# Attention and two expert layers on one core: q turned in pairs of 64-row transposes, half of k's exps taken from PSUM, first loads reordered

## The chip, the core and the metric

The kernel runs on one core of a Trainium2 chip. The core has a matrix engine (TensorE, here PE; PEld is its loading of stationary operands), VectorE (DVE), ScalarE (ACT), GpSimd (POOL) and SyncE (SP), each with an instruction stream of its own that is worked off strictly in order; they meet only at semaphores. Sixteen DMA engines move data between HBM and the on-chip memory SBUF. PE writes its results to PSUM, eight banks of 128 x 512 fp32, from where DVE and ACT read them. The metric is the device time of one execution in microseconds (us); lower is better.

## The reference

Three stages in a row, all in fp32, with 8 batches, 8 heads, 576 positions, 64 values per head. The change touches the first alone:

```python
def phi(x):
    proj = np.einsum('bhsd,df->bhsf', x, w_phi)                   # 128 features
    proj = proj - np.max(np.abs(proj), axis=-1, keepdims=True)
    return np.concatenate([np.exp(proj), np.exp(-proj)], axis=-1)
q_p, k_p = (phi(q), phi(k))
kv = np.einsum('bhsf,bhsd->bhfd', k_p, v)
z = np.sum(k_p, axis=2)
num = np.einsum('bhsf,bhfd->bhsd', q_p, kv)
den = np.einsum('bhsf,bhf->bhs', q_p, z)[..., None] + 1e-06
return (num / den).astype(np.float32)
```

Its result passes through two expert layers (a mixing of each position with the one before it, four matrix products with w_k, w_v, w_r and w_val, a convolution of width 5, a product with w_out).

## The kernel before

The attention runs in 32 steps, `j = 2n + p`. A group `n` holds four heads: a step works on two of them, `ab` = 0 and 1, which lie on partitions 0 to 63 and 64 to 127 of the loaded q and k, and on their first 512 positions in 4 chunks of 128. The last 64 positions of all four heads are done once per group (`tails`, `turn_tails`). For each step:

- `proj` (L630, called by `q_proj` and `k_proj`): PE multiplies 4 chunks of each head with w_phi, the two heads on the two 64-row halves of the array at once, each into a PSUM bank of its own (`project`, L618). `centre` (L621) then has DVE take the largest absolute value of each row (L624) and subtract it (L626) into SBUF.
- for k, ACT takes exp of the centred values and of their negatives, 512 columns at a time (L670), into `ek`.
- for q, `turn` (L677) transposes each head's 4 chunks on the whole 128x128 array (L683), one bank per head, and ACT takes the two exps on the way from PSUM to SBUF (L687), into `qe`.
- `kv` (L704): PE sums exp(k) times v (with a column of ones for z) on the two 64-column halves of the array (L724); ACT copies the result (L369).
- `num` (L734), once per head: PE multiplies q's exps with that state (L758), again on column halves; ACT copies; `scale` divides on POOL and DVE; `back` (L788) transposes the result on the whole array (L798).

Meanwhile the weights of the expert layers are fetched, rearranged by ACT, DVE and POOL and written back to HBM (`convert`). After the last step come the expert layers, with products on the whole array (L900).

In the trace every fp32 product of the attention shows as two weight loads and two matmuls, a transpose as one of each; so the 4 chunks of two heads are 16 pieces of L618, and a turn of one head 4 of L683.

The order on each engine is not written out. `Order.run` (L166) gives every task a duration and a due time: it is `j` plus a number from the table `T` (L33). For each engine it takes the task that can start first, by the durations written in the code (0.84 for a projection, `t_act(n)` for ACT and so on; `ENTER` is what it books for a change of the array's shape, `SOON` and `EARLY` how far it goes to avoid one). It also chooses the PSUM banks. The instructions are then issued in that order; on the chip each engine goes through its list and waits where a semaphore is not yet there. PE's order, for example, can't change at run time.

The first loads: SP issues q's three pieces for group 0 (512, 128 and 512 columns), then v; ACT issues w_phi in two halves and then k's three pieces (`load_t`, L584, with `by="ACT"`). PE runs 8 products on the identity as a warm-up until they land.

Of the kernel before, what the change touches and what calls it, by code (L numbers as in the profile page):

```python
# [22 lines left out]
QW = 1152  # L23
# [9 lines left out]
T = dict(load_q=-1.89, load_k=-2.75, load_v=-2.03, tails=-1.0, q_proj=-1.5, k_proj=-1.505, turn=-0.592, sums=-0.5, num=0.4, back=1.049, finish=1.9, convert=1.09, ones=-1.23)  # L33
FROM, TO = 0, 27.43
# [9 lines left out]
DMA_END = 2.5  # L44
# [3 lines left out]
KV = 0.117  # L48
ENTER = {"rows": 0.2, "columns": 0.14, "all": 0.15}
SOON, EARLY = 0.6, 0.405  # L50
# [241 lines left out]
def build(ctx, tc, qt, kt, vv, wphi, mu, wk, wr, wv, wval, cw, wout, out):  # L292
# [49 lines left out]
    def ps(tag):  # L342
        return Buf(tag, None)
# [240 lines left out]
    def load_t(n, dst, src, nm):  # L584

        f = sb(nm + "h", [128, QW])
        cuts = [(0, 512), (1024, QW), (512, 1024)] if n == 0 else [(0, QW)]
        for i, cut in enumerate(cuts):
# [41 lines left out]
    def proj(x, j, tag):  # L630
# [8 lines left out]
        add("PE", 0.84, lambda: project(bs, x[n], [p * 512 + 128 * i for i in range(4)], 0),  # L639
# [3 lines left out]
        return [d[:2] for d in ds]  # L643

    def tails(j):
# [8 lines left out]
        add("PE", 0.42, go, r=cols_of(qs[n], n, 2) + cols_of(ks[n], n, 2) + [("wph", 0), ("wph", 1)], w=bs, new=bs, split="rows")  # L654
# [9 lines left out]
    def k_proj(j):  # L664
        ds = proj(ks, j, "d")
        for ab in range(2):
            d, tok = ds[ab]
            e = st[j]["ek", ab] = sb("ek", [128, 4, 2, 128])
            for half in range(2):
                add("ACT", t_act(512, False), lambda d=d, e=e, half=half: act(  # L670
                    out=e[:, :, half], in_=d(), func=AF.Exp, scale=-1.0 if half else 1.0),
                    r=[tok], w=[(e, half)] if j or ab + half < 2 else [(e, half), "first"], new=[] if half else [e])

# [3 lines left out]
    def turn(j, ab):  # L677

        s = st[j]
        if ab == 0:  # L680
            s["qe"] = sb("qe", [128, 2, 2, 512])
# [4 lines left out]
        for half in range(2):  # L686
            add("ACT", t_act(512), lambda half=half: act(  # L687
                out=e[:, ab, half, :], in_=b[:], func=AF.Exp, scale=-1.0 if half else 1.0),
                r=[b], w=[(e, ab, half)], new=[] if ab or half else [e])
# [44 lines left out]
    def num(j, ab):  # L734
# [9 lines left out]
        reads = [(e, ab, 0), (e, ab, 1), s["kv"]]  # L744
# [551 lines left out]

    for j in range(NP):
        n, p = divmod(j, 2)
        st[j] = {}
        if p == 0:  # L1300
            due(j + T["load_q"] if n else -8.0, load_t, n, qs, qt, "q")
            due(j + T["load_k"] if n else -7.0, load_t, n, ks, kt, "k")
            due(j + T["load_v"] if n else -6.0, load_v, n)
            due(j + T["ones"] if n else -4.0, ones, n)
            due(j + T["tails"], tails, j)
        due(j + T["q_proj"], q_proj, j)
        due(j + T["k_proj"], k_proj, j)
        if p == 0:
            due(j + T["turn"] + 0.4, turn_tails, n)
# [64 lines left out]
```

## Time and profile before

| | |
|---|---|
| median of 3 runs | 957.3 us (952.86 to 958.5) |
| profiled execution | 957.62 us, of which the span of the core is 955.8 us |
| TensorE clock granted over the span | 1.000 of full speed |
| PE busy | 933.7 us (98%) |
| DVE, ACT, POOL busy | 831.3 (87%), 690.6 (72%), 204.3 us (21%) |

The attention fills the first third of the span: POOL, which works only there, is idle from the 14th of the page's 40 slices on, and PE issues its first product of the expert layers at 305.36 us. A busy PE means that a matmul is somewhere in its pipeline, so two pieces overlap in the busy sums, and their cost is better read from when the next piece begins (the chain in order of time). ACT's and DVE's neighbours overlap too: two in a row take less than twice the time of one.

### The profile page before, as it was taken

How to read it: one execution, taken by the hardware profiler on the slowest of the kernel's cores; microseconds unless marked ns; L12 is line 12 of the kernel's file. 1: busy time of each engine (PE TensorE's matmuls, PEld its weight loads, DVE VectorE, ACT ScalarE, POOL GpSimd, SP SyncE). 2: the span in 40 equal slices, each digit the busy share in tenths (PEclk: the TensorE clock that was granted, in tenths of full speed). 3: DMA queues.
4: the chain of work that ended last, by engine and by line, in shares of the span. 5: the costliest groups of instructions: out<-in, count | busy, mean ns of one | idle time of the engine just before them, and what ended most of it. 6: DMA issues, size and time to landing. Idle time of an engine off the chain costs nothing.

```text
span 955.8 us, 27000 instructions
## 1 busy us (share of the span) xinstructions
PE 933.7 (98%) x11264; PEld 906.8 (95%) x11264; DVE 831.3 (87%) x1276; ACT 690.6 (72%) x1253; POOL 204.3 (21%) x360
## 2 busy tenths in 40 slices
PE   6999999999999999999999999999999999999997
PEld 6899989988898999999999999999999999999997
DVE  5899989989887799879978978997997897899695
ACT  4768778777677987668857947876885794787453
POOL 0296978777683000000000000000000000000000
PEclk9999999999999999999999999999999999999999
DMA  7465589889857475588378577748837856754883
GB/s 242 155 203 184 175 272 306 258 283 305 286 170 263 155 275 204 182 274 295 118 284 287 189 259 260 246 181 288 293 128 275 285 200 252 267 193 165 285 306 138
DMA packets 79770, 224.27 MB, mean 235 GB/s; under 512 B 10144, under 2 KB 35104, under 8 KB 66592
## 3 DMA queue, kind: packets, MB, share of 16 engines
q1 hardware_dynamic: 70352, 212.45, 64.9%
q10 hardware_dynamic: 9296, 10.09, 3.0%
q8 instruction: 89, 1.46, 0.6%
q14 instruction: 33, 0.27, 0.1%
HBM read 186.87 MB, written 35.65 MB: 233 GB/s over the span
## 4 chain that ended last, share of the span: by engine, by line
PE 88%; DVE 5%; ACT 4%; DMA 2%; issue 1%; ACTq 0%; DVEq 0%
PE c L900 58%; PE b L724 8%; PE b L618 8%; PE b L758 8%; PE b L683 4%; PE b L798 2%; DVE ops L372 1%; ACT ops L878 1%; DMA out<-y 1%; DVE x L869 1%; DMA ops<-in_kt 1%; ACT y L878 0%; ACT x L878 0%; ACT g L878 0%; PE b L696 0%
## 5 line engine op out<-in xcount | busy, mean ns | idle before, releaser
L900 PE MATMUL c<-ops,u 128*128 128x288 f32 x1968 | 275.5, 295 | 4.1 <-DVE ops L372 2.5
L900 PEld LDWEIGHTS c<-ops,u 128*128 128x128 f32 x1968 | 266.2, 188 | 6.1 <-DVE ops L372 3.4
L900 PE MATMUL c<-ops,wkt 128*128 128x288 f32 x1344 | 180.0, 295 | 0.7 <-ACT c L1021 0.7
L900 PEld LDWEIGHTS c<-ops,wkt 128*128 128x128 f32 x1344 | 178.3, 188 | 1.1 <-ACT c L1021 0.9
L624 DVE TENSOR_REDUCE dd<-b 128x4 f32<-128x512 f32 (+1 forms) x160 | 95.0, 627 | 25.8 <-PE b L618 24.4
L872 DVE SCALAR_TENSOR_TENSOR g<-x,cwt,g 128x576 f32<-128x576 f32 x128 | 102.1, 815 | 0.0
L878 ACT ACTIVATE ops<-k 128x576 fp32r<-128x576 f32 x96 | 65.3, 680 | 46.2 <-PE c L900 43.2
L372 DVE TENSOR_TENSOR ops<-k,ops 128x576 fp32r<-128x576 f32 x96 | 71.7, 755 | 25.2 <-ACT ops L878 25.0
L618 PE MATMUL b<-wph,ops 64*128 64x128 f32 x1152 | 83.2, 287 | 6.3 <-DMA ops<-in_kt 4.7
L618 PEld LDWEIGHTS b<-wph,ops 64*128 64x128 f32 x1152 | 71.2, 191 | 14.6 <-issue 5.5
L687 ACT ACTIVATE y<-b 128x512 f32<-128x512 f32 x128 | 69.9, 599 | 13.4 <-PE b L683 12.3
L758 PE MATMUL b<-g,y 128*64 128x65 f32 x2176 | 74.9, 223 | 1.4 <-issue 1.4
L758 PEld LDWEIGHTS b<-g,y 128*64 128x64 f32 x2176 | 68.0, 137 | 7.3 <-issue 3.4
L369 ACT ACTIVATE x<-b 128x260 f32<-128x260 f32 (+3 forms) x96 | 40.3, 424 | 38.9 <-PE b L758 27.2
L878 ACT ACTIVATE k<-k 128x576 f32<-128x576 f32 x98 | 63.3, 679 | 0.9 <-DVE k L869 0.5
L878 ACT ACTIVATE sp<-c 128x576 f32<-128x576 f32 x50 | 32.4, 648 | 43.3 <-PE c L900 43.3
L626 DVE TENSOR_TENSOR k<-b,dd 128x512 f32<-128x512 f32 (+1 forms) x84 | 49.5, 616 | 0.0
L900 PE MATMUL c<-y,u 128*128 128x288 f32 x336 | 48.0, 294 | 0.0
L900 PE MATMUL c<-y,xf 128*128 128x288 f32 x336 | 46.8, 295 | 0.0
L900 PEld LDWEIGHTS c<-y,u 128*128 128x128 f32 x336 | 45.7, 188 | 0.0
L900 PEld LDWEIGHTS c<-y,xf 128*128 128x128 f32 x336 | 45.3, 188 | 0.0
L878 ACT ACTIVATE k<-c 128x576 f32<-128x576 f32 x64 | 41.3, 646 | 5.0 <-PE c L900 4.5
(148 smaller groups left out, 1795.2 us busy)
## 6 DMA issues: line engine op xcount, KB each, us to landing
u<-ws SPq DMA_DIRECT2D x86, 1024.0 KB, 5.4
xf<-ws SPq DMA_DIRECT2D x16, 1024.0 KB, 6.5
ws<-dd SPq DMA_DIRECT2D x28, 512.0 KB, 6.2
dd<-ws SPq DMA_DIRECT2D x24, 512.0 KB, 5.7
ot<-ws SPq DMA_DIRECT2D x20, 512.0 KB, 5.9
xs<-x SPq DMA_DIRECT2D x16, 576.0 KB, 4.3
xx<-xs SPq DMA_DIRECT2D x8, 1152.0 KB, 7.6
out<-y ACTq DMA_DIRECT2D x32, 288.0 KB, 5.4
```

The costliest lines, as they stand in the source:

```text
L369: act(out=out, in_=x, func=AF.Copy)
L372: eng.tensor_tensor(out=out, in0=x, in1=hi.bitcast(F32), op=ALU.subtract)
L618: mm(out=bs[ab][:, (at + i) * 128:(at + i + 1) * 128], lhsT=x[r, c:c + 128], rhs=wph[r], start=True, stop=True)
L624: add("DVE", t_dve(128 * n), lambda: nc.vector.tensor_reduce(out=m[:, 0:n, 0], in_=b3[:, 0:n], axis=AX.X, op=ALU.max, apply_absolute_value ...
L626: add("DVE", t_dve(128 * n), lambda: tt(out=d[0](), in0=b3[:, 0:n], in1=m[:, 0:n].to_broadcast([128, n, 128]), op=ALU.subtract), r=[b, m], ...
L683: add("PE", 0.109 * 4, lambda: [nc.tensor.transpose(out=b[:, c * 128:c * 128 + 128], in_=d()[:, c], identity=ident) for c in range(4)], r= ...
L687: add("ACT", t_act(512), lambda half=half: act(out=e[:, ab, half, :], in_=b[:], func=AF.Exp, scale=-1.0 if half else 1.0), r=[b], w=[(e, a ...
L724: mm(out=b[y, o:o + 65], lhsT=lhs[:, y], rhs=vt[:, a:a + 65], start=(k == 0), stop=(c == 3), skip_group_check=True)
L758: mm(out=b[rows, at:at + 65], lhsT=lhs, rhs=a[:, o:o + 65], start=(k == 0), stop=(half == 1), skip_group_check=True)
L872: add("DVE", d_time(n) + 0.06, lambda: stt(out=out(), in0=x(), scalar=scalar(), in1=y(), op0=ALU.mult, op1=ALU.add), r=r, w=w)
L878: act(out=out(), in_=x(), func=func, **more)
L900: mm(out=o[:, half, 0:TB], lhsT=a, rhs=mov[b][c], start=first and k == 0, stop=last and k == n - 1, skip_group_check=True)
```

## The change

Three edits of the code, and a new table of due times with them.

1. `turn` handles both heads at once. A head's chunk, 128 positions by 128 features, is transposed in two halves of 64 positions (`y`), the lower 64 partitions on the lower half of the array's rows, the upper on the upper half. The halves go to two banks: bank `y` gets that half of both heads. There are 16 transposes of 64 x 128 instead of 8 of 128 x 128; the exps are still four of 512 columns, now by half instead of by head, so `num` of one head needs all four. The turn waits for both heads of q.
2. `proj_k` replaces `k_proj`. For head `ab` = 0 nothing changes. For `ab` = 1 (`ASIDE`) DVE takes the maximum and its negative (4 columns), and does not subtract: ACT reads the projection from PSUM and adds the maximum as a per-partition bias, so the exps go chunk by chunk, 8 of 128 columns in place of 2 of 512.
3. The three pieces of k and q for group 0 are issued on SP, alternating, k first; v comes between the first two pieces and the third.

```diff
-T = dict(load_q=-1.89, load_k=-2.75, load_v=-2.03, tails=-1.0, q_proj=-1.5, k_proj=-1.505, turn=-0.592, ...
+T = dict(load_q=-1.801, load_k=-2.905, load_v=-2.62, tails=-0.979, q_proj=-1.5, k_proj=-1.505, turn=-0.592,
...
-DMA_END = 2.5
+DMA_END = 2.574
...
+TURN = 0.47
+ASIDE = ((0, 1), (1, 1))
 ENTER = {"rows": 0.2, "columns": 0.14, "all": 0.15}
-SOON, EARLY = 0.6, 0.405
+SOON, EARLY = 0.211, 0.35
...
         for i, cut in enumerate(cuts):
+            if n == 0 and i != part:
+                continue
             c, wide = slice(*cut), cut[1] - cut[0]
-            load(lambda c=c: f[:, c], lambda c=c: src[n, :, c], wide * 512, w=[(f, i)], new=[] if i else [f],
-                 by="ACT" if (n, nm) == (0, "k") else "SP")
+            load(lambda c=c: f[:, c], lambda c=c: src[n, :, c], wide * 512, w=[(f, i)], new=[] if i else [f])
...
-        add("PE", 0.84, lambda: project(bs, x[n], [p * 512 + 128 * i for i in range(4)], 0),
+        add("PE", 0.893, lambda: project(bs, x[n], [p * 512 + 128 * i for i in range(4)], 0),
...
+    def proj_k(j):
...
+        for ab in range(2):
+            e = st[j]["ek", ab] = sb("ek", [128, 4, 2, 128])
+            if (p, ab) in ASIDE:
+                apart(bs[ab], e, j, ab)
+            else:
...
+    def apart(b, e, j, ab):
+        m, b3 = sb("m", [128, 2, 4]), Part(lambda: b[:].rearrange("p (c f) -> p c f", f=128))
+        add("DVE", t_dve(512), lambda: nc.vector.tensor_reduce(
+            out=m[:, 0], in_=b3[:], axis=AX.X, op=ALU.max, apply_absolute_value=True), r=[b], w=[m], new=[m])
+        add("DVE", 0.15, lambda: nc.vector.tensor_scalar(
+            out=m[:, 1], in0=m[:, 0], scalar1=-1.0, scalar2=None, op0=ALU.mult), w=[m])
+        for half in range(2):
+            def go(half=half):
+                for c in range(4):
+                    act(out=e[:, c, half], in_=b3[:, c], func=AF.Exp, scale=-1.0 if half else 1.0,
+                        bias=m[:, 1 - half, c:c + 1])
+            add("ACT", 4 * t_act(128) - 0.3, go, r=[b, m], w=[(e, half)] if j or ab + half < 2 else [(e, half), "first"],
+                new=[] if half else [e])
...
-    def turn(j, ab):
+    def turn(j):
...
-        b, (d, tok), e = ps("qp"), s["dq"][ab], s["qe"]
-        add("PE", 0.109 * 4, lambda: [nc.tensor.transpose(
-            out=b[:, c * 128:c * 128 + 128], in_=d()[:, c], identity=ident) for c in range(4)],
-            r=[tok], w=[b], new=[b])
...
+        bs, ds = [ps("qp"), ps("qp")], s["dq"]
+        e = s["qe"] = sb("qe", [128, 2, 2, 512])
+
+        def go():
+            for ab in range(2):
+                for c in range(4):
+                    for y in range(2):
+                        r, k = slice(64 * y, 64 * y + 64), 256 * ab + 64 * c
+                        nc.tensor.transpose(out=bs[y][:, k:k + 64], in_=ds[ab][0]()[r, c], identity=ident[r, r])
+
+        add("PE", TURN, go, r=[tok for _, tok in ds], w=bs, new=bs, split="rows")
...
-        reads = [(e, ab, 0), (e, ab, 1), s["kv"]]
+        reads = [(e, y, half) for y in range(2) for half in range(2)] + [s["kv"]]
...
-                lhs = e[:, h, half, 128 * c + 64 * y:128 * c + 64 * y + 64] if c is not None else ex[:, half, h, rows]
+                lhs = e[:, y, half, 256 * h + 64 * c:256 * h + 64 * c + 64] if c is not None else ex[:, half, h, rows]
...
-            due(j + T["load_q"] if n else -8.0, load_t, n, qs, qt, "q")
-            due(j + T["load_k"] if n else -7.0, load_t, n, ks, kt, "k")
...
+                for i in range(3):
+                    due(-8.0 + 1.5 * i, load_t, n, qs, qt, "q", i)
+                    due(-8.5 + 1.5 * i, load_t, n, ks, kt, "k", i)
+                due(-5.7, load_v, n)
```

With the new durations and due times the planner sets another order. PE in the middle of the attention, before: `b_..` are PSUM banks, `wph,ops` is w_phi with the loaded q or k, `ident,sp` the turn of one head, `u,k` and the like the state product, `ident,ot` the transposes of `back`.

```order
L618 MATMUL b_82<-wph,ops 128x128
L618 MATMUL b_90<-wph,ops 128x128
L683 MATMUL b_83<-ident,sp 128x128 x4
L724 MATMUL b_89<-u_72,k_69 64x65 x8
L724 MATMUL b_89<-u_72,u_70 64x65 x16
L724 MATMUL b_89<-u_72,g 64x65 x16
L798 MATMUL b_91<-ident,ot 128x128 x4
L798 MATMUL b_81<-ident,ot 128x128
L683 MATMUL b_88<-ident,sp 128x128 x4
L618 MATMUL b_84<-wph,ops 128x128
```

The two heads' turns stand apart, each on the whole array, one of them alone between a projection and a state product. PE in the middle of the attention, after (`g,y` is `num`, `ident,k` the turn of the tails):

```order
L760 MATMUL b_89<-u_72,k_69 64x65 x24
L760 MATMUL b_89<-u_72,u_70 64x65 x16
L794 MATMUL b_90<-g,y 64x65 x24
L732 MATMUL b_84<-ident,k_69 128x128 x2
L794 MATMUL b_83<-g,y 64x65 x16
L627 MATMUL b_88<-wph,ops 128x128
L627 MATMUL b_89<-wph,ops 128x128
...
L718 MATMUL b_90<-ident,sp 128x64
L718 MATMUL b_82<-ident,sp 128x64
```

Both heads' turn (16 rows of L718, alternating between two banks) now stands in one place, here directly behind a projection that uses the same row halves. ACT in the first steps, before: `u<-k` and `k<-k` are exps of k, `g<-b` and `x<-b` copies of kv and num, `y<-b` exps of q.

```order
L670 ACTIVATE k_69<-k_69 128x4x128 x2
L670 ACTIVATE u_70<-k_69 128x4x128 x2
L369 ACTIVATE g<-b_84 128x260
L369 ACTIVATE x_74<-b_90 128x260
L687 ACTIVATE y<-b_88 128x512 x2
```

A step's four exps of k are four instructions. ACT in the first steps, after:

```order
L667 ACTIVATE k_69<-k_69 128x4x128 x2
L680 ACTIVATE u_70<-b_91,dd 128x128 x8
L375 ACTIVATE g<-b_90 128x260
L375 ACTIVATE x_74<-b_82 128x260
L416 ACTIVATE xf<-xx 128x512
L723 ACTIVATE y<-b_81 128x512 x2
```

The second pair has become eight that read a PSUM bank, ahead of the same copies. SP's first issues, after (`in_kt`, `in_qt`, `in_vv` are k, q and v in HBM; before, SP has q's three pieces first, then v, and k's stand behind w_phi on ACT):

```order
L396 DMA ops<-in_kt 128x512
L396 DMA ops<-in_qt 128x512
L396 DMA ops<-in_kt 128x128
L396 DMA ops<-in_qt 128x128
L396 DMA u_71<-in_vv 128x1040
L396 DMA u_71<-in_vv 64x2x64 x2
L396 DMA ops<-in_kt 128x512
L396 DMA ops<-in_qt 128x512
```

k's first piece has moved from the third place of ACT's queue to the first of SP's, and the third pieces of k and q stand behind v.

## Rows read from the trace of the kernel before

**Rows 1.** the page, parts 1 and 4: busy time and the chain by engine:
```profile
PE 933.7 (98%) x11264; PEld 906.8 (95%) x11264; DVE 831.3 (87%) x1276; ACT 690.6 (72%) x1253; POOL 204.3 (21%) x360
...
PE 88%; DVE 5%; ACT 4%; DMA 2%; issue 1%; ACTq 0%; DVEq 0%
```

**Rows 2.** windows: us, busy us (instructions) of PE, PEld, DVE, ACT, POOL; clock:
```profile
25.00:305.00 280.00, 275.06 (x6227) 252.12 (x6228) 251.70 (x467) 209.67 (x460) 199.49 (x337) 1.00 0.74 242
```

**Rows 3.** waits of PE, 25:305 us (total, times, longest), first and last of three:
```profile
PE b L758 <- issue: 2.9, 2, 1.5
...
PE b L724 <- issue: 1.4, 2, 0.8
```

**Rows 4.** chain in order of time: start us, us, line and pieces:
```profile
1.95 7.71 DMA ops<-in_kt
...
94.79 2.33 PE b L724 x80
...
98.06 1.02 PE b L683 x8
99.08 1.99 PE b L618 x32
...
143.96 2.48 PE b L724 x80
146.45 0.59 PE b L683 x4
...
148.77 1.09 PE b L618 x16
...
155.60 2.02 PE b L758 x64
```

**Rows 5.** timeline, start and first expert product: start us, us, engine:
```profile
0.72 1.19 ACTq L390 DMA_DIRECT2D wph<-in_wphi  x2
...
1.34 3.78 PE L566 MATMUL b<-ident 128*128 128x128 f32 x16 [1.34 <-POOL ident masks.py:199]
...
9.80 5.00 PE L618 MATMUL b<-wph,ops 64*128 64x128 f32 x56 [4.68 <-DMA ops<-in_kt]
...
305.36 1.86 PE L900 MATMUL c<-ops,wkt 128*128 128x288 f32 x12
```

**Rows 6.** groups by line and form, 25 to 305 us, weight loads:
```profile
L758 PEld LDWEIGHTS b<-g,y 128*64 128x64 f32 x2165 | 67.6, 137 | 7.2 <-issue 3.4 <-ACT x L369 0.2 <-ACT x L700 0.2
L618 PEld LDWEIGHTS b<-wph,ops 64*128 64x128 f32 x1048 | 63.6, 187 | 9.4 <-issue 5.3 <-ACT x L369 1.8 <-ACT k L670 0.2
...
L683 PEld LDWEIGHTS b<-ident,sp 128*128 128x128 f32 x248 | 27.1, 141 | 3.1
```

**Rows 7.** DMA issues, 0 to 25 us: KB each, median us to landing:
```profile
ops<-in_qt SPq DMA_DIRECT2D x2, 256.0 KB, 3.7
```

**Rows 8.** groups on DVE and ACT, last two from 305 us on:
```profile
L626 DVE TENSOR_TENSOR k<-b,dd 128x512 f32<-128x512 f32 x59 | 38.7, 679 | 0.0
...
L670 ACT ACTIVATE u<-k 128x512 f32<-128x512 f32 x60 | 34.6, 628 | 2.0 <-DVE k L626 2.0
...
L369 ACT ACTIVATE x<-b 128x128 f32<-128x128 f32 x15 | 4.1, 276 | 1.5 <-PE b L798 1.5
...
L878 ACT ACTIVATE k<-k 128x576 f32<-128x576 f32 x98 | 63.3, 679 | 0.9 <-DVE k L869 0.5
...
L878 ACT ACTIVATE dd<-xx,mut 128x576 f32<-128x576 f32 x32 | 23.6, 766 | 0.0
```

**Rows 9.** timelines of DVE and of ACT in one step:
```profile
111.10 0.27 DVE L777 RECIPROCAL g<-dd 128x8 f32<-128x8 f32 x2
...
126.16 1.14 ACT L670 ACTIVATE u<-k 128x512 f32<-128x512 f32 x2
```

**Rows 10.** waits of ACT, 25 to 305 us, the two largest:
```profile
ACT x L369 <- PE b L758: 24.6, 28, 1.9
ACT y L687 <- PE b L683: 11.3, 21, 2.5
```

More of the change, by code (lines that the diff above doesn't have):

```diff
@@ L30 @@
 LEAST, MOST = pattern((896 + 128) << 20), pattern(((1150 + 128) << 20) | 0xFFFFF)
[L33 to L34 removed]
+T = dict(load_q=-1.801, load_k=-2.905, load_v=-2.62, tails=-0.979, q_proj=-1.5, k_proj=-1.505, turn=-0.592,
+         sums=-0.5, num=0.4, back=1.078, finish=1.924, convert=1.09, ones=-2.309, turn_x=0.434, turn_step=0.308,
+         num_step=0.301, scale=0.526)
+ODD = dict(q_proj=0.038, k_proj=-0.02, turn=0.0, sums=0.0, num=-0.15, back=0.0)
+FIRST = dict(q_proj=0.649, k_proj=0.226, tails=0.378, turn=0.044, sums=0.765)
+FROM, TO = 0, 27.413
 LAST = ("pj", "qp", "kv")
@@ L643, in proj @@
         return [d[:2] for d in ds]
+    def proj_k(j):
+        n, p = divmod(j, 2)
+        bs = [ps("pj"), ps("pj")]
+        add("PE", 0.893, lambda: project(bs, ks[n], [p * 512 + 128 * i for i in range(4)], 0),
+            r=cols_of(ks[n], n, p) + [("wph", 0), ("wph", 1)], w=bs, new=bs, split="rows")
+        for ab in range(2):
[3 more added lines that the diff above has]
+            else:
+                d = sb("d", [128, 4, 128])
+                centre(bs[ab], (lambda d=d: d[:], d, [d]), 4)
+                for half in range(2):
+                    add("ACT", t_act(512, False), lambda d=d, e=e, half=half: act(
+                        out=e[:, :, half], in_=d[:], func=AF.Exp, scale=-1.0 if half else 1.0),
+                        r=[d], w=[(e, half)] if j or ab + half < 2 else [(e, half), "first"], new=[] if half else [e])
+    def apart(b, e, j, ab):
[4 more added lines that the diff above has]
+            out=m[:, 1], in0=m[:, 0], scalar1=-1.0, scalar2=None, op0=ALU.mult), w=[m])
+        for half in range(2):
+            def go(half=half):
[4 more added lines that the diff above has]
+                new=[] if half else [e])
     def tails(j):
@@ L652, in go @@
                 project(bs, x[n], [1024], i)
-        add("PE", 0.42, go, r=cols_of(qs[n], n, 2) + cols_of(ks[n], n, 2) + [("wph", 0), ("wph", 1)], w=bs, new=bs, split="rows")
+        add("PE", 0.446, go, r=cols_of(qs[n], n, 2) + cols_of(ks[n], n, 2) + [("wph", 0), ("wph", 1)], w=bs, new=bs, split="rows")
         for ab in range(2):
@@ L662, in tails @@
                 r=[(d, 0), (d, 1)], w=[(e, half)], new=[] if half else [e])
[L664 to L672, printed above, removed]
     def q_proj(j):
         st[j]["dq"] = proj(qs, j, "dq")
-    def turn(j, ab):
+    def turn(j):
         s = st[j]
-        if ab == 0:
-            s["qe"] = sb("qe", [128, 2, 2, 512])
-        b, (d, tok), e = ps("qp"), s["dq"][ab], s["qe"]
-        add("PE", 0.109 * 4, lambda: [nc.tensor.transpose(
-            out=b[:, c * 128:c * 128 + 128], in_=d()[:, c], identity=ident) for c in range(4)],
-            r=[tok], w=[b], new=[b])
[L686 to L689, printed above, removed]
+        bs, ds = [ps("qp"), ps("qp")], s["dq"]
[7 more added lines that the diff above has]
+        add("PE", TURN, go, r=[tok for _, tok in ds], w=bs, new=bs, split="rows")
+        for y in range(2):
+            for half in range(2):
+                add("ACT", t_act(512), lambda y=y, half=half: act(
+                    out=e[:, y, half, :], in_=bs[y][:], func=AF.Exp, scale=-1.0 if half else 1.0),
+                    r=[bs[y]], w=[(e, y, half)], new=[] if y or half else [e])
     def turn_tails(n):
```

36 lines of the change are left out of this document (22 added, 14 removed).

## The prediction, made before the changed kernel had run

> **What bounds the kernel now.** I read the page first: TensorE is busy for 98% of the span and holds 88% of the chain that ended last; DVE has 5% and ACT 4% of that chain [rows 1]. The busy share alone would prove little, so the next view is the table by stage [rows 2]. From 25 to 305 us (attention and the weight conversion) PE is busy for 275.06 of 280 us, DVE for 251.70 (90%), ACT for 209.67 (75%), POOL for 199.49 (71%). From 305 us on only the expert layers run, which the change doesn't touch. Third, PE's waits in the attention stretch [rows 3]: three groups of at most 2.9 us, all "issue", so no engine and no load that the trace shows holds PE up there. Fourth, the chain in order of time [rows 4]: piece follows piece on PE, a transpose behind a state product, a projection behind a transpose. So attention is bound by the sum of its PE pieces, and what is taken out of a piece shortens the stage, as long as DVE and ACT keep up. Only the first 10 us are different: PE stands for 4.68 us for the first load of k [rows 5].
>
> The profiled execution took 957.62 us, a span of 955.8 plus 1.8 around it; the median of the runs shown is 957.3. The sum below is made against 957.6, and the two agree within 0.3 us.
>
> **Term 1, the turn of q.** Before, each of the 32 steps turns two heads by 8 transposes of 128x128. Eight in a row take 1.02 us and four 0.59, so one takes 0.43 / 4 = 0.1075 and a step's eight 0.86 us [rows 4]. After, a step has 16 transposes of 64 rows, alternating between the two row halves and two banks: 8 pairs. No row of before has such a pair, and two rows bound it. A pair of products side by side with 65 moving columns costs (2.02 - 0.15) / 32 = 0.058 us (64 pieces of L758, less the entry priced in term 2) [rows 4]. A pair of projections, with the same 64x128 weights but 128 moving columns, costs (1.99 - 1.09) / 8 = 0.1125 us (32 against 16 pieces of L618) [rows 4]. The new pair moves 64 columns, as the first, and loads 128 weight columns, as the second. Which of the two decides is told by the loads: 128 columns take 187 ns in a projection, 64 columns 137 ns in a product, but a transpose's 128 columns take 141 ns [rows 6]. That is as short as the load which a pair of 0.058 us hides. I therefore take 8 x 0.058 = 0.47 us, with 0.90 as the other end. Saving: 0.86 - 0.47 = 0.39 us a step, 12.5 us in 32 steps; at the other end a loss of 1.3.
>
> The Trainium skill (TensorE: Matmul & The Clock Gate, section LDWEIGHTS) speaks against this: a weight load costs its columns divided by 1.2 GHz whatever its rows, about 107 ns for 128 columns. By it, as an estimate, 8 pairs cost 0.85 us and the turn gains nothing. The trace has 187 ns for 128 columns and 137 for 64, which is the rule's step of some 50 ns; the 141 of a transpose with 128 columns is not [rows 6].
>
> **Term 2, changes of the array's shape.** Work on 64-row halves, on 64-column halves and on the whole array alternates, and each change costs: into row halves 1.09 - 8 x 0.1125 = 0.19 us, into column halves 2.48 - 2.33 = 0.15, into the whole array 0.59 - 0.43 = 0.16 [rows 4]. The turn now has the projections' shape and mostly stands beside one, as the order rows of PE show. Counted over both programs' PE order, whole-array groups fall from 68 to 46, row groups rise from 60 to 65 and column groups from 66 to 73: -22 x 0.16 + 5 x 0.19 + 7 x 0.15 = -1.5 us.
>
> **Term 3, the first loads.** k's first piece goes out at 1.95 us on ACT's queue, behind two loads of w_phi and beside q's and v's, and takes 7.71 us; PE begins at 9.80 [rows 4, 5]. After, it is the first issue on SP, where q's first piece stands now, which with its like has a median of 3.7 us to landing [rows 7]. Issued at about 0.7 it is there at 4.4; w_phi's second half, whose two issues begin at 0.72 and last 1.19 us together [rows 5], at 1.3 + 3.7 = 5.0 by the same time; the warm-up ends at 5.1 [rows 5]. PE begins 4.7 us sooner. What follows is DVE's: two maxima and two subtractions per projection, and both heads of q must be centred before the first turn, so all of it moves with the start. The second pieces of k and q go out later than now, as eighth and ninth on SP, but the first turn waits for DVE's eight operations longer than for them. I take -4.7; bounds -2 (a late second piece holds PE) and -6 (DVE's shorter work on k counts here too).
>
> **Term 4, k's exps.** In each step one of the two heads loses its subtraction on DVE, 679 ns alone [rows 8]; the new negation of 4 columns is nearest to a reciprocal of 8, of which two take 0.27 us [rows 9], so 0.1 to 0.2. DVE: -0.5 us a step. PE covers that before and after: worth nothing by itself. ACT loses two exps of 512 columns from SBUF, 1.14 us for two in a row where one alone takes 0.628 [rows 8, 9]: neighbours overlap by 0.11 and cost 0.52 each, 1.04 together. It gains eight of 128 columns from PSUM with a per-partition operand. One of 128 columns alone takes 0.276 [rows 8], in a row 0.276 - 0.11 = 0.16; a per-partition operand makes a 576-column form 766 instead of 679 ns: +0.09 [rows 8]. Eight take 8 x 0.25 = 2.0 us; ACT: +0.96 us a step. The other end is no overlap, 0.366 each, 2.9 us.
>
> Does it fit? L683's 248 transposes in the stretch are 31 steps [rows 6]: a step has 9.03 us, of which ACT 6.76, DVE 8.12, POOL 6.44 [rows 2]. After terms 1 and 2 a step has 9.03 - 0.44 = 8.6; ACT needs 7.7, DVE 7.6, POOL 6.4. ACT goes from 75% to 90%, where DVE is now, and DVE at 90% cost PE no wait that the profile names [rows 3]. So the exps stay hidden, but closely. One thing gets late: the list that sets the order books 0.81 less 0.1 for four of them, 0.71, where I price 1.0, so ACT falls 0.56 us behind its plan in each step and must make it up from time in which it waits today, 36 us in its two largest groups alone [rows 10]. Behind the exps on ACT stand the copies of kv and num and q's exps; on PE, kv waits for the exps, and a projection's second bank is released by ACT instead of DVE. I put 2 us on this; bounds 0 and 32 x 0.56 = 18.
>
> **Sum**: -12.5 - 1.5 - 4.7 + 2 = -16.7; 957.6 - 16.7 = 940.9, said as 941.
>
> **Rivals.** *A: a new pair costs what a projection's pair costs, or its two run one behind the other*: 0.90 us a step. For it: 64x128 weights as in L618, and no row shows transposes side by side. Against: the 141 ns, and that L618's pairs do overlap. Time: 957.6 + 1.3 - 1.5 - 4.7 = 953, within 1%.
>
> *B: ACT's shortfall against its plan reaches PE.* For it: 0.56 us a step, on queues that are strictly in order. Against: PE waits for nobody although DVE is at 90% [rows 2, 3]. In full: 957.6 - 18.7 + 18 = 957; half of it 948. Mostly within 1%.
>
> *C, the other side: the eight small exps do not overlap, and ACT becomes the bound.* Then ACT needs 6.76 - 1.04 + 2.9 = 8.6 us a step, as much as PE. If its two largest waits, 36 us or 1.16 a step, stay, since they are for PE's own results [rows 10], a step takes 9.76: 957.6 - 4.7 + 32 x 0.73 = 976. It decides, as slower by over 1%, from 9.5 us a step. Against: two exps of 512 columns overlap by 0.11 us [rows 8, 9].
>
> **Chances.** Forecast 0.64, A 0.15, B 0.14, C 0.07. About 1% is what a measurement of this kernel can tell from no change. Faster by more, under 947.8: the forecast and a little of B, 0.66. Within 1%: A, most of B and a slow edge of the forecast, 0.27. Slower: C, 0.07. The range reaches from 935 (term 3 at -6, no new wait, a pair a little under 0.058) to 954, which takes in A and half of B; the forecast's own is 935 to 948.
>
> **What would show it.** Sixteen new transposes in the chain at about 0.47 us beside a projection, 0.66 alone, and their weight loads near 140 ns: term 1; over 0.9: A. The first projection near 5 us: term 3. The first product of the expert layers near 305.36 - 16.7 = 288.7 us [rows 5]. The small exps starting 0.25 us apart: term 4; 0.36: C. PE's waits in attention under 8 us and none of them large and for ACT: no B; many waits for the exps at state products or projections: B. From the first product of the expert layers to the end both kernels should take the same 650 us; if not, the whole sum is at fault.

## The result and the profile after

The changed kernel took 948.14 us (median of 8 runs, 946.83 to 951.36) beside 957.42 us of the kernel before (8 runs, 952.86 to 961.72): a ratio of 0.9909, 95% interval 0.9884 to 0.9935, 9.3 us less by the medians. That is inside the range, 7 us above the 941 that was named, and just within the 1% that the text called no change, to which it gave a chance of 0.27 against 0.66 for more. The sign was right; of the 16.7 us forecast a little over half came.

| | before | after |
|---|---|---|
| profiled execution (its span) | 957.62 us (955.8) | 947.15 us (945.3) |
| first projection on PE | 9.80 us | 5.05 us |
| first product of the expert layers | 305.36 us | 295.95 us |
| from there to the span's end | 650.4 us | 649.3 us |

The page of after, parts 1 and 4, and the window of [rows 2] (us, busy us and instructions of PE, PEld, DVE, ACT, POOL, granted clock):

```profile
PE 924.8 (98%) x11520; PEld 899.3 (95%) x11520; DVE 824.3 (87%) x1276; ACT 717.3 (76%) x1445; POOL 210.8 (22%) x360
...
PE 81%; ACT 7%; DVE 4%; issue 1%; ACTq 0%
```

```profile
25.00:305.00 280.00, 270.57 (x6375) 248.69 (x6371) 248.20 (x467) 237.67 (x640) 208.48 (x341) 0.99 0.73 243
```

Against [rows 1] PE's busy share is still 98%, but its part of the chain fell from 88% to 81%, and ACT's rose from 4% to 7%: the path now leaves PE more often. In the window ACT has 28 us more than in [rows 2], DVE 3.5 less although more of the program passes in the same 280 us. Where the path leaves PE is told by PE's waits of after, from the first projection to the first expert product (total us, times, longest; "issue" is time in which the engine waited for nothing that the profile shows):

```profile
PE b L794 <- ACT g L375: 4.4, 8, 1.0
PE b L627 <- ACT u L680: 1.5, 1, 1.5
PE b L718 <- DVE sp L635: 1.4, 2, 1.0
PE b L760 <- issue: 1.0, 2, 0.8
PE b L627 <- issue: 0.9, 1, 0.9
PE b L794 <- issue: 0.5, 1, 0.5
PE b L794 <- ACT y L723: 0.3, 2, 0.2
PE b L760 <- ACT k L700: 0.3, 1, 0.3
```

Before, the same stretch had the three groups of "issue" of [rows 3], 5.9 us in all, and one wait for DVE ahead of 25 us:

```profile
PE b L683 <- DVE sp L626: 1.4, 1, 1.4
```

So PE's waits went from 7.3 to 10.3 us. Now the largest group is `num` (L794) waiting for the copy of kv (L375), which stands on ACT directly behind the eight small exps (L680), and a projection waits 1.5 us for such exps itself. ACT's four lines sum to 6.5 us, where before had none; "issue" has gone down from 5.9 to 2.4.

The start and the end of the attention, in the timeline of PE and of SP's queue (start us, us, engine, line):

```profile
0.72 0.38 SPq L396 DMA_DIRECT2D ops<-in_kt  x1
...
1.34 3.78 PE L572 MATMUL b<-ident 128*128 128x128 f32 x16 [1.34 <-POOL ident masks.py:199]
5.05 2.29 PE L627 MATMUL b<-wph,ops 64*128 64x128 f32 x18
...
295.95 2.65 PE L936 MATMUL c<-ops,wkt 128*128 128x288 f32 x18
```

k's first piece goes out at 0.72 us and PE passes from the warm-up into the projection with no wait; in [rows 5] it stood 4.68 us for that load. And the turn, in the chain in order of time (start us, us, line, pieces) and in PE's weight loads from 25 to 295 us:

```profile
86.45 1.09 PE b L627 x16
87.55 0.49 PE b L718 x16
...
117.30 0.64 PE b L718 x16
117.94 2.48 PE b L760 x80
```

```profile
L627 PEld LDWEIGHTS b<-wph,ops 64*128 64x128 f32 x1040 | 63.4, 187 | 7.2 <-issue 2.4 <-ACT u L680 2.1 <-ACT k L667 0.3
...
L718 PEld LDWEIGHTS b<-ident,sp 64*128 64x128 f32 x464 | 17.8, 138 | 3.2 <-DVE xf L908 1.1 <-DVE sp L635 0.5 <-issue 0.3
```

Sixteen small transposes take 0.49 us behind a projection and 0.64 elsewhere (0.69 in four places), where eight full ones took 0.86 and more [rows 4]; their loads take 138 ns although they have the same 64x128 form as the projection's 187.

### The profile page after: what moved, and what is told of

It is laid out like the page before. It is cut to its first block, busy times and chain, and to the rows that moved or that the text cites. A ratio compares the mean times of both kernels' runs of the same rounds, so it can differ in the third digit from the quotient of the medians.

```text
span 945.3 us, 27713 instructions
## 1 busy us (share of the span) xinstructions
PE 924.8 (98%) x11520; PEld 899.3 (95%) x11520; DVE 824.3 (87%) x1276; ACT 717.3 (76%) x1445; POOL 210.8 (22%) x360
## 4 chain that ended last, share of the span: by engine, by line
PE 81%; ACT 7%; DVE 4%; issue 1%; ACTq 0%
PE c L936 63%; PE b L794 6%; PE b L760 5%; PE b L627 4%; PE b L834 2%; ACT y L723 1%; PE b L718 1%; ACT ops L914 1%; ACT u L680 1%; DVE ops L378 1%; DVE x L905 1%; ACT x L914 0%; ACT k L667 0%; PE b L732 0%; ACT x L375 0%
## 5 line engine op out<-in xcount | busy, mean ns | idle before, releaser
L633 DVE TENSOR_REDUCE dd<-b 128x4 f32<-128x512 f32 (+1 forms) x128 | 76.1, 614 | 25.7 <-PE b L627 24.4
L794 PE MATMUL b<-g,y 128*64 128x65 f32 x2176 | 77.2, 225 | 5.2 <-ACT g L375 4.4
L794 PEld LDWEIGHTS b<-g,y 128*64 128x64 f32 x2176 | 69.4, 139 | 12.6 <-ACT g L375 6.1
L723 ACT ACTIVATE y<-b 128x512 f32<-128x512 f32 x128 | 69.1, 615 | 13.3 <-PE b L718 11.0
L375 ACT ACTIVATE x<-b 128x260 f32<-128x260 f32 (+3 forms) x96 | 42.8, 464 | 16.0 <-PE b L834 7.7
L914 ACT ACTIVATE ops<-x 128x576 fp32r<-128x576 f32 x48 | 32.5, 678 | 13.1 <-PE c L936 8.2
```

What stands on the lines that cost most here:

```text
L375: act(out=out, in_=x, func=AF.Copy)
L633: add("DVE", t_dve(128 * n), lambda: nc.vector.tensor_reduce(out=m[:, 0:n, 0], in_=b3[:, 0:n], axis=AX.X, op=ALU.max, apply_absolute_value ...
L723: add("ACT", t_act(512), lambda y=y, half=half: act(out=e[:, y, half, :], in_=bs[y][:], func=AF.Exp, scale=-1.0 if half else 1.0), r=[bs[y ...
L794: mm(out=b[rows, at:at + 65], lhsT=lhs, rhs=a[:, o:o + 65], start=(k == 0), stop=(half == 1), skip_group_check=True)
L914: act(out=out(), in_=x(), func=func, **more)
```

## The experiments

All are variants of the changed kernel, except one. "The changed kernel's list" means that no task has another place on the engines than in the changed kernel; where a duration, a task's engine or a load is changed in the code that the planner sees, it makes a new list, and then most of PE's pieces stand in another place or another bank too. Theory W, which came out of the waits above, says: ACT is late against its plan, PE waits for it, and that is what ate the gain. Theory D says that DVE's relief or PE's own pieces set the time and ACT is covered. Ratios are to the kernel before, run beside each.

**The small exps without their bias.** The same list, the same eight exps; they leave out the maximum of k's second head, so only their time counts.

```diff
                 for c in range(4):
-                    act(out=e[:, c, half], in_=b3[:, c], func=AF.Exp, scale=-1.0 if half else 1.0,
-                        bias=m[:, 1 - half, c:c + 1])
+                    act(out=e[:, c, half], in_=b3[:, c], func=AF.Exp, scale=-1.0 if half else 1.0)
```

> The changed kernel in the same order on every engine; the eight small exps of a step carry no per-partition bias (this leaves the maximum of k's second head out of the result). Theory W (PE's new waits come from ACT being slower than the list books, 2.15 us for eight exps in a row against 1.42): the exps start about 0.16 us apart instead of 0.25, ACT gains about 0.7 us a step, and PE's waits between its first projection and the first product of the expert layers fall from 16.9 us to about 10: about 942 us. Rival D (the waits come from the new turn, which needs both heads of q and whose result num needs whole, or from DVE): the waits stay, 947 to 948 us.

Measured: 943.51 us, ratio 0.9857 (0.9833 to 0.9881). The small exps start 0.157 us apart instead of 0.249 (median over the start-to-start distances of L680), 0.74 us a step. PE's waits:

```profile
PE b L759 <- issue: 4.1, 4, 2.1
PE b L793 <- issue: 2.6, 6, 0.9
PE b L793 <- ACT g L375: 1.5, 2, 1.0
PE b L717 <- DVE sp L635: 0.9, 2, 0.5
```

The copy of kv holds PE up for 1.5 us instead of 4.4, no projection waits for the exps any more, and the time falls by 4.6 us: W. Of the 6.5 us of waits for ACT 2.1 are left. That PE's waits would fall in all was missed: "issue" rose from 2.4 to 7.3, and this view sums to 11.1 us where the changed kernel has 10.3.

**The subtraction back on DVE, in place.** The changed kernel's list; DVE subtracts in the PSUM bank where it made the negative, and ACT takes two exps of 512 columns from there.

```diff
-        add("DVE", 0.15, lambda: nc.vector.tensor_scalar(
-            out=m[:, 1], in0=m[:, 0], scalar1=-1.0, scalar2=None, op0=ALU.mult), w=[m])
+        add("DVE", 0.15, lambda: tt(
+            out=b3[:], in0=b3[:], in1=m[:, 0].rearrange("p (c x) -> p c x", x=1).to_broadcast([128, 4, 128]),
+            op=ALU.subtract), w=[m])
...
-                for c in range(4):
-                    act(out=e[:, c, half], in_=b3[:, c], func=AF.Exp, scale=-1.0 if half else 1.0,
-                        bias=m[:, 1 - half, c:c + 1])
+                act(out=e[:, :, half], in_=b3[:], func=AF.Exp, scale=-1.0 if half else 1.0)
```

> The changed kernel in its own order on every engine; where DVE took the negative of the maximum (0.16 us) it now subtracts the maximum in place in the PSUM bank (0.60 us in a row), and ACT takes two exps of 512 columns from that bank instead of eight of 128. Per step ACT gets about 1.1 us back and DVE 0.44 us more. Theory W (ACT's lateness is what PE waits for): 941 to 944 us, as with the exps without bias, or better. Rival E (DVE is the next bound, so what the edit took off DVE is what it was worth): 950 to 954 us, as with the subtraction planned anew, and PE's and ACT's waits name DVE.

Measured: 944.39 us, ratio 0.9866 (0.9834 to 0.9897), 3.7 us under the changed kernel: the fastest version that computes everything. Its window from 25 to 295 us, then the changed kernel's:

```profile
25.00:295.00 270.00, 259.93 (x6317) 238.94 (x6312) 250.57 (x459) 201.58 (x452) 207.01 (x336) 1.00 0.75 250
```

```profile
25.00:295.00 270.00, 260.57 (x6279) 238.76 (x6276) 239.66 (x454) 229.40 (x625) 204.21 (x335) 0.99 0.75 248
```

DVE is busy for 250.6 of 270 us, 93%, more than in either kernel, and no wait of PE names these subtractions; ACT waits 3.0 us for them, where in the changed kernel it waits 2.6 for the negative; ACT gets back 28 us. Of its PE waits:

```profile
PE b L793 <- issue: 5.4, 7, 1.5
PE b L717 <- issue: 1.9, 2, 1.3
PE b L793 <- ACT g L375: 1.4, 2, 1.0
```

All eleven runs of this kernel and of the one without bias (942.73 to 946.37) lie below all fourteen of the changed kernel, those of the next experiment included (946.83 to 951.36). So half of k's exps is the part of the change that costs: it took load off the engine with cover and put it on the one whose lateness reaches PE. Here too "issue" is large, 8.6 us in all, where the changed kernel had 2.4 and the kernel before 5.9.

**The changed kernel once more.** The medians of these two lie 4.6 and 3.7 us under the changed kernel's, but their profiled executions (945.52 and 946.37 us) only 1.6 and 0.8 under its profiled one, so it was run again.

> The changed kernel itself, once more, with a second profile. The two kernels without the small exps' price (no bias, and the subtraction back on DVE) were 3.7 and 4.6 us under the changed kernel's median, but their profiled executions only 0.8 and 1.6 us under its profiled one. Theory W (the small exps cost PE about 4 us): the median stays at 947 to 949, ratio near 0.991, and PE's waits for ACT in this second execution are again 6 to 10 us. If the difference lay in the executions that happened to be drawn: 944 to 946, and ACT's waits may be smaller.

Measured: 949.49 us (6 runs, 948.37 to 950.0), ratio 0.9905 (0.9873 to 0.9937). Its largest waits of PE:

```profile
PE b L794 <- ACT g L375: 3.6, 6, 1.0
PE b L760 <- issue: 2.9, 2, 1.4
PE b L794 <- issue: 2.0, 2, 1.3
PE b L627 <- ACT u L680: 1.5, 1, 1.5
```

The waits for ACT come again, in the same places and of the same size (5.9 us in all, 6.5 before); "issue" does not, it is 4.9 instead of 2.4, and the first expert product comes at 298.31 instead of 295.95. So the 4 to 5 us between it and the two kernels above are no accident of the executions drawn, while single profiles of one kernel differ by 2 us.

**The small exps made dearer.** The scale too is read from a column of SBUF that holds 1 or -1; same list.

```diff
+    signs = const.tile([128, 2], F32, name="signs")
...
-                    act(out=e[:, c, half], in_=b3[:, c], func=AF.Exp, scale=-1.0 if half else 1.0,
+                    act(out=e[:, c, half], in_=b3[:, c], func=AF.Exp, scale=signs[:, half:half + 1],
```

> The changed kernel with the dose turned up where the third experiment turned it down: each of the eight small exps of a step reads its scale too from a column of SBUF (plus or minus one), which makes the exps dearer by what a per-partition operand costs, near 0.09 us each by what the bias cost, 0.7 us a step. Same order on every engine. Theory W (PE waits for what ACT is late with): ACT's waits of PE grow by 4 to 8 us from about 8, 952 to 956 us. Rival (ACT's load is covered, and the gain without the bias came from elsewhere): about 948.

Measured: 961.42 us, ratio 1.0052 (1.0034 to 1.007), 13 us above the changed kernel and slower than before. The exps start 0.343 us apart, so ACT has 0.75 us a step more, and PE's waits for ACT sum to 19.1 us, the three largest being

```profile
PE b L798 <- ACT g L375: 12.6, 16, 1.9
PE b L627 <- ACT u L684: 2.9, 4, 1.8
PE b L722 <- ACT u L684: 1.5, 2, 0.9
```

The wait for the copy of kv is three times the changed kernel's. W has both signs now: 0.74 us a step less on ACT gains 4.6 us, 0.75 more costs 13.3. The size was missed (952 to 956 expected): the cost is not proportional, it grew faster than what was added to ACT.

**The pairs taken apart.** The sixteen transposes in another order, first the eight of the lower row half, then the eight of the upper.

```diff
-            for ab in range(2):
-                for c in range(4):
-                    for y in range(2):
+            for y in range(2):
+                for ab in range(2):
+                    for c in range(4):
```

> The changed kernel with q's sixteen transposes of a step given out in another order: first the eight of the lower half of the rows, then the eight of the upper half, so that neighbours no longer stand in different halves. Everything else keeps its place. Theory S (the pairs run side by side, which is term 1 of the prediction): a step's turn goes back from 0.49 us to about 0.9, the eight pairs' price twice; 32 steps by 0.41 are 13 us, about 961 us. Rival A (two small transposes never overlap, and the turn is short for another reason): about 948, no change, and the turn stays at 0.49.

Measured: 952.03 us, ratio 0.9954 (0.9935 to 0.9974); 3.9 us lost, where S said 13 and A nothing. The chain has the turn at

```profile
116.10 0.94 PE b L718 x16
...
235.66 0.79 PE b L718 x16
```

0.94 us alone and 0.79 behind a projection, against 0.64 and 0.49: the pairs do overlap, and the edit costs 0.30 us a step, 9.6 us in 32. Rival A falls. S's step of 0.41 was missed because the edit took only five of the eight pairs apart. PE is given eight lower pieces and then eight upper ones, but it did not start them in that order: in the trace 97 starts of L718, three a step, lie less than 0.02 us behind the one before, and where a projection follows, its first piece mostly starts ahead of the turn's last three. So the order of PE's list, which the text ahead of the prediction calls fixed, does not hold between the two halves of the rows. A piece without such a neighbour stands 0.062 us from the next (median), as long as a whole pair in the changed kernel; five pairs apart are 5 x 0.062 = 0.31 us, which is what was measured.

Of the 9.6 us that PE has to do more, 3.9 reached the end. Waits took up a part of the rest: PE waits less for ACT (3.8 us instead of 6.5) and for DVE (0.6 instead of 1.4), but 1.9 us for a piece of k, for which the changed kernel waits 0 and 0.3 us in its two profiles; in all it is 8.9 us against 10.3. Where the other 4 us went is not shown.

**The first loads as before.** The changed kernel's list with q's, k's and w_phi's old issues ahead of it.

```diff
-        load(lambda a=a: wph[64 * a:64 * a + 64], lambda: wphi, 32768, w=[("wph", a)], by="ACT")
+        add("ACT", 0.1, lambda: None, w=[("wph", a)], dma=32768)
...
+            if n == 0:
+                add("SP", 0.62, lambda: None, w=[(f, i)], new=[] if i else [f], dma=wide * 512)
+                continue
...
+    for a in range(2):
+        nc.scalar.dma_start(out=wph[64 * a:64 * a + 64], in_=wphi)
+    for q, src, slot in ((nc.sync, qt, "qh0"), (nc.scalar, kt, "kh0")):
+        f = view(*PLACE[slot], [128, QW])
+        for a, b in ((0, 512), (1024, QW), (512, 1024)):
+            q.dma_start(out=f[:, a:b], in_=src[0, :, a:b])
```

> The changed kernel with the first loads issued as before (q on SP ahead of v, k on ACT behind w_phi) and the same order of everything else. If the loads are worth just the start: the first projection moves from 5.05 us to between 7.7 and 9.8, and the time is 948.1 + 2.7 to 4.7 = 951 to 953 us. If the 957.5 of the version planned anew was the loads' own doing: 956 to 958 us. If the start is made up for by DVE's list: 948 to 950 us.

Measured: 951.39 us, ratio 0.9936 (0.991 to 0.9962). The loads are worth 3.3 us in the time by the two medians; the interval, 5 us wide, doesn't tell that from the 4.7 that was priced. The start itself moves by all of it, 9.72 against 5.05, and the first expert product of the profiled execution by 4.4 us, 300.32 against 295.95:

```profile
9.72 1.65 PE L630 MATMUL b<-wph,ops 64*128 64x128 f32 x12 [4.92 <-DMA ops<-in_kt]
...
300.32 1.85 PE L939 MATMUL c<-ops,wkt 128*128 128x288 f32 x12
```

**Kernels whose list was made anew.** Four runs were meant to isolate a part and isolated nothing, because the planner set another order with the edit. Three of them came out above every time that had been expected.

The old loads, by the planner's own due times:

```diff
-            load(lambda c=c: f[:, c], lambda c=c: src[n, :, c], wide * 512, w=[(f, i)], new=[] if i else [f])
+            load(lambda c=c: f[:, c], lambda c=c: src[n, :, c], wide * 512, w=[(f, i)], new=[] if i else [f],
+                 by="ACT" if (n, nm) == (0, "k") else "SP")
...
-                    due(-8.0 + 1.5 * i, load_t, n, qs, qt, "q", i)
-                    due(-8.5 + 1.5 * i, load_t, n, ks, kt, "k", i)
-                due(-5.7, load_v, n)
+                    due(-8.0, load_t, n, qs, qt, "q", i)
+                for i in range(3):
+                    due(-7.0, load_t, n, ks, kt, "k", i)
+                due(-6.0, load_v, n)
```

> The changed kernel with the first loads as before (q on SP ahead of v, k on ACT behind w_phi), planned anew. If the loads are worth what the first projection gains (5.05 against 9.80 us): 948.1 + 4.7 = 952.9 us, with the first projection near 9.8 us. If the start is made up for later (DVE works off the same list): 948 to 950 us.

Measured: 957.50 us, ratio 1.0005 (0.999 to 1.0019), 6 us above the same edit in the changed kernel's list.

The subtraction of both heads on DVE, into SBUF, as before the change:

```diff
-ASIDE = ((0, 1), (1, 1))
+ASIDE = ()
```

> The changed kernel with all of k's heads subtracted on DVE as before (two exps of 512 columns from SBUF), planned anew: the turn in pairs and the new loads alone. Theory W: ACT gets back 0.96 us a step and PE's waits go to 9 to 11 us, 941 to 944 us, which is the forecast of 941 without the part on k's exps. Rival D: the waits stay, 947 us or more. Rival E (DVE, which gets 0.5 us a step back, is the next bound at 8.1 of 8.6 us): 948 to 952 us, with PE waiting for DVE.

Measured: 953.93 us, ratio 0.9972 (0.9957 to 0.9988), against 944.39 for nearly the same work in the changed kernel's list.

The true price booked:

```diff
-            add("ACT", 4 * t_act(128) - 0.3, go, r=[b, m], ...
+            add("ACT", 1.1, go, r=[b, m], ...
```

> The changed kernel with one number of its planner corrected: four small exps are booked at 1.1 us instead of 0.81, so 1.0 after the overlap; nothing else is changed, but the order is planned anew. Theory W: the plan now allows for ACT, PE's waits fall by 4 to 6 us, about 943 us. Rival D: no effect beyond the scatter of a new order, 946 to 950 us. If ACT is simply too full, a correct plan can't help and the time stays as well; then e3_nobias still falls.

Measured: 951.75 us, ratio 0.9933 (0.9911 to 0.9955). Booking the true price gained nothing that can be told from scatter; the interval overlaps the changed kernel's.

The copy of kv, booked and run on DVE:

```diff
-        add("ACT", t_act(260), lambda: copy(a[:], b[:, 0:260]), r=[b], w=[a], new=[a])
+        add("DVE", t_dve(260), lambda: nc.vector.tensor_copy(out=a[:], in_=b[:, 0:260]), r=[b], w=[a], new=[a])
```

> The changed kernel with the copy of the state product (kv, 260 columns, 0.27 us on ACT in a row) moved to DVE (0.35 to 0.42), planned anew. In the changed kernel PE waits 4.4 us for this copy, behind the small exps. Theory W: these waits go, 943 to 946 us. Rival E: DVE can't take it, 949 to 953 us.

Measured: 954.59 us, ratio 0.9968 (0.9942 to 0.9995).

To separate the edit from the order, the last of them was built again with the booking left on ACT, so that every task stays where the changed kernel has it and only the copies run on DVE:

```diff
-        add("ACT", t_act(260), lambda: copy(a[:], b[:, 0:260]), r=[b], w=[a], new=[a])
+        add("ACT", t_act(260), lambda: nc.vector.tensor_copy(out=a[:], in_=b[:, 0:260]), r=[b], w=[a], new=[a])
```

> The changed kernel with the copy of kv moved from ACT to DVE, as in an earlier run, but this time the list is made as before, so PE, SP and all other work keep the changed kernel's order and only these 33 copies stand on another engine. ACT loses about 0.43 us a step, DVE gains about as much. Theory W (PE waits for what ACT is late with, above all this copy: 4.4 us in 8 waits) with theory O (the earlier run was slow because its list was made anew): 944 to 947. If the move itself is bad (DVE, then near 92% busy, holds PE up in ACT's place): 950 to 956, as in the earlier run.

Measured: 946.49 us, ratio 0.9892 (0.9861 to 0.9923): 8.1 us under the same edit with a new list. PE's wait for the copy, 4.4 us in the changed kernel, is

```profile
PE b L794 <- issue: 2.8, 5, 1.0
...
PE b L794 <- DVE g L768: 0.7, 1, 0.7
PE b L627 <- ACT u L680: 0.6, 1, 0.6
```

0.7 us. So these four tell what a list is worth, 6 to 10 us where the pair was run, and nothing on the parts of the change. That the copy on DVE beats the changed kernel is not settled: the intervals overlap.

**The loads alone**, in the kernel before (its list, too, is made anew):

```diff
...
+            if n == 0 and i != part:
+                continue
...
-            load(lambda c=c: f[:, c], lambda c=c: src[n, :, c], wide * 512, w=[(f, i)], new=[] if i else [f],
-                 by="ACT" if (n, nm) == (0, "k") else "SP")
+            load(lambda c=c: f[:, c], lambda c=c: src[n, :, c], wide * 512, w=[(f, i)], new=[] if i else [f])
...
+                for i in range(3):
+                    due(-8.0 + 1.5 * i, load_t, n, qs, qt, "q", i)
+                    due(-8.5 + 1.5 * i, load_t, n, ks, kt, "k", i)
+            due(j + T["load_v"] if n else -5.7, load_v, n)
...
```

> The kernel before with the new order of the first loads alone, planned anew by its own table. By the step on the loads: 957.4 - 4.7 = 952.7 us, first projection near 5 us, and the first product of the expert layers near 300.6. If the new plan eats it: 955 to 958 us.

Measured: 955.46 us, ratio 0.9976 (0.995 to 1.0001); PE starts at 4.71 us. Inconclusive: the interval reaches from no gain to 4.8 us, all that was forecast for the loads.

## Why the prediction was right and wrong

To compare with the sum, the distance from each start on PE to the next, between the first projection and the first expert product, was booked to the kind of the earlier instruction, to a change of shape, or, where it was over the kind's usual distance by a stall, to the waits. The stretch went from 295.6 to 290.9 us: the turn -9.5, changes of shape -3.3, `back` -1.9, state, `num`, projections and the tails' turn together +2.1, the waits +7.9. Where a slow piece ends and a stall begins is a choice. A recount that books to the waits only what a distance has beyond its kind's usual one, from 0.06 us on, has -13.2 for turn, changes and `back` together, +5.8 for the waits and +2.6 for the rest; the profile's view of waits rises by 3.0 (7.3 to 10.3). That the waits grew is common to all three, the size is not; and 1.5 us of the stretch after are a fall of the clock (last section).

**Terms 1 and 2, the turn and the shapes: right.** Forecast -12.5 and -1.5, together -14.0; the account has -9.5, -3.3 and -1.9, -14.7 (-13.2 in the recount). A pair stands 0.062 us apart (two starts on, median), as L758's 0.058 and not as L618's 0.1125; loads 138 ns. The choice of the row by the weight load's duration was the right one, and rival A is refuted by the pairs taken apart. How the gain divides between the two terms can't be read from this account: the last piece before a change of shape is booked whole to the change, so a piece moves from its kind to the changes when its neighbour does. `back`'s -1.9 is of that sort: 21 of its 33 groups stood directly before a turn of the same shape, and afterwards none does. The rule that a load takes its columns divided by 1.2 GHz (the Trainium skill, "TensorE: Matmul & The Clock Gate", section LDWEIGHTS), which gave 0.85 us a step, is contradicted by the 138 and 187 ns of two loads of one form.

**Term 3, the loads: right.** Forecast -4.7; the first projection moved by 4.75 us, and with the old loads in the same list the first expert product comes 4.4 us later. In the time it is 3.3 us, which that run can't tell from 4.7.

**Term 4, k's exps: the step that failed.** The price was right: eight at 0.25 us, measured 0.249. So was "DVE: worth nothing by itself": with 93% on DVE no wait of PE for k's subtractions appeared. What failed was the size of what follows, "I put 2 us on this; bounds 0 and 18". (Of its working, two times 1.0 less 0.71 is 0.58 and not 0.56, which changes nothing.) Undoing the part in the same list gives back 3.7 us (4.6 without the bias), and PE's waits for ACT are 6.5 and 5.9 us in two executions. The text's sign against rival B, waits of PE under 8 us and none of them large and for ACT, did not come. The argument that stood behind the 2 was that ACT could make up its 0.56 us a step out of 36 us of waiting. For the most part it did: of ACT's waits between 25 and 295 us, the two of [rows 10] are in the changed kernel

```profile
ACT y L723 <- PE b L718: 11.0, 12, 1.8
...
ACT x L375 <- PE b L794: 6.2, 11, 1.0
```

17 us instead of 36, and all its waits for PE sum to 28.8 us where they are 48.8 with the subtraction back on DVE. That is 20 of the 28 us that the small exps add. What the argument missed is that ACT must be late with nothing that PE wants at once: behind the small exps stands the copy of kv, and PE's next `num` needs it. So the evidence that "DVE at 90% cost PE no wait" did not carry over to ACT. This is rival B, in a mild form. Its 948 for "half of it" is the time measured, but by luck: only 4 to 5 of B's 9 us came by its mechanism.

**What was left out: the other waits.** 3.7 us for term 4 don't explain all: with the part undone, the kernel is at 944.4, still 5.5 above 957.6 - 18.7. By the view of waits PE waits 13.0 us there against 7.3 before: 8.6 "issue" (5.9 before), 2.0 for ACT, 1.4 for a later piece of k, 1.0 for q's subtractions. That is 5.7 more, about what is missing; it is one execution, though, and the slowest of six. The sum took every us out of a PE piece as a us of the stage and put no other wait into it but ACT's; at 98% busy that was too much. Whether "issue" stalls grow because PE waits less for ACT is not shown: they are 8.6 and 7.3 us in the two kernels that relieve ACT of the exps' price and 2.4 and 4.9 in the changed kernel, but 4.6 where the copy of kv moved to DVE, and 8.5 beside 6.0 us of waits for ACT where both heads are subtracted under a new list.

**What no run separates: the order.** The change came with a new table of due times, so with a list of its own, and the sum priced of it only the changes of shape. A list made anew moved other kernels here by 6 to 10 us. The kernel before was not run with the new table alone, so how much of the 9.3 us gained, or of the 7.4 missing, is the order's own stays open.

**Rival C fell:** the exps overlap, 0.249 us apart. **From the first expert product on** both take 650 us, 650.4 and 649.3, as the text required of its own sum. The 0.66 on faster by over 1% rested on term 4 being small and on every other wait staying as it was; the margin under 947.8 was 7 us, and 7.4 of the 16.7 us did not come.

## What to carry to other kernels

A busy share doesn't say which engine can take load: ask what stands on it one step ahead of the bound engine's next piece, and put new work on the engine whose results are wanted late, even at 93%, rather than on the one at 75% whose copies are wanted at once. When the order comes from a planner, test a part in the frozen order; a list made anew moved the time by 6 to 10 us here, more than undoing any one part did. And count a gain on an engine at 98% in full only where the waits that appear next have been priced.

## What the runs showed of the hardware that was not expected

- **Pieces of the two row halves start out of the order in which PE is given them.** With the pairs taken apart, three pieces a step still start less than 0.02 us behind another, though all eight lower ones stand ahead of the upper ones. A half transpose takes 0.062 us to the next start, alone or with one of the other half beside it; a full one takes 0.109.
- **Each per-partition operand costs a small exp 0.09 us**: 0.157, 0.249 and 0.343 us from start to start with none, one and two. The Trainium skill ("ScalarE: Activation LUTs", section What ACT_TABLE_LOAD costs) states 93 ns for each; the trace agrees.
- **PE's "issue" stalls follow instruction loads.** In the fourteen profiled executions 84 stalls of PE in the attention, behind the first loads, have no semaphore behind them (0.46 us and more from start to start, up to 2.3). Every one ended 1.2 to 1.6 us after a 16 KB packet on the queue of instructions had finished; such packets come 5.6 to 5.9 us apart, so by chance it would be about one in fourteen. One in the changed kernel, in the timeline of PE:

```profile
141.66 0.49 PE L627 MATMUL b<-wph,ops 64*128 64x128 f32 x2
143.03 1.04 PE L627 MATMUL b<-wph,ops 64*128 64x128 f32 x13 [0.88 <-issue]
```

  and what the DMA view has for 140 to 142 us, where the queue q1 fills 97% of the engines' time and one instruction packet runs between:

```profile
q1 hardware_dynamic: 285, 0.70, 97.2%
q8 instruction: 1, 0.02, 3.0%
```

  The Trainium skill ("Runtime: NRT & Kernel Launch", section Instruction fetch mechanics) says that each sequencer fetches its program in blocks of 16 KiB over a DMA queue of its own, and that this is mostly hidden; here it is not always: the "issue" waits are 1.7 to 9.7 us of an attention stage, and differ in two executions of one kernel (2.4 and 4.9).
- **Behind one short wait the clock fell.** In the first profile of after PE waited 1.54 us for the exps until 112.31 us, and at 113.19 us the granted clock fell to half (1.2 GHz) for 3.4 us. Windows of that place (the clock stands behind POOL's column):

```profile
108.00:113.00 5.00, 3.46 (x88) 3.20 (x85) 4.63 (x12) 5.00 (x16) 2.99 (x6) 1.00 0.49 136
113.00:117.00 4.00, 4.00 (x48) 3.33 (x45) 1.89 (x3) 2.17 (x6) 3.92 (x8) 0.57 0.73 236
117.00:125.00 8.00, 8.00 (x215) 7.27 (x213) 7.23 (x13) 7.17 (x21) 4.78 (x8) 1.00 0.53 166
```

  From the end of the wait to the next turn PE took 4.92 us, and 3.46 for the same pieces in the second profile, which has the same wait (1.53 us) and no fall: 1.5 us lost. So such a fall does not always come, and that the wait caused it is not shown.
